# Queries turned on TensorE, key groups of nine tiles, exponentials summed on GpSimd, shared load buffers and a new searched order

## The chip, the cores and the metric

The kernel runs on one core of one Trainium2 chip. The metric is the device time of one execution in microseconds; the number quoted for a kernel is the median of its runs. The span that a profile covers is about 2 us shorter than the time of the same run, because the time includes what lies outside the first and last recorded instruction.

## The reference

Four batches of 12,544 rows of 128 numbers go through "agent attention" (49 agent rows stand between queries and keys), and the result through a feed-forward stage that takes the maximum of three linear layers of width 768.

```python
def _attn_ref(q, k, v, agents):           # q, k, v: (4, 12544, 128); agents: (4, 49, 128)
    ...                                    # sm(a, b): softmax over b of a @ b.T / sqrt(128)
    agent_v = sm(agents, k) @ v            # 49 x 128 per batch: needs ALL keys of the batch
    return sm(q, agents) @ agent_v

def _moe_ref(x, w1, w2, w3, w_out):        # x: (50176, 128), w1..w3: 128 x 768, w_out: 768 x 128
    h = np.maximum(np.maximum(x @ w1, x @ w2), x @ w3)
    return h @ w_out
```

The result of a query needs the finished `agent_v` of its batch. So keys of batch b+1 are worked on while queries of batch b are, and each batch change has to wait for a small calculation that ends the keys.

## The kernel before

A tile is 128 rows. Queries come in 49 groups of eight tiles, keys in groups of eight. For each batch a matrix `G` is made once from `agent_v` and the differences of the weights. After that a query group needs only: scores against 49 agents, one exponential (`e_q`), 12 products of `e_q` with `G` into three large PSUM buffers (`uv`), maxima of pairs of them (`a_sb` on ACT, `r` on DVE), the output products and a scale by the reciprocal sums.

The program is one list of small steps, each with a number that says when it is issued. One query group takes 6.0 of these numbers, whatever the time is. The table `KEY` holds the numbers inside a group; it was found by a search.

```python
    KEY = {"s": -0.90, "ex": -0.41, "u0": 0.94, ..., "rec": 3.76, ..., "sc1": 13.45}
    loads = ctx.enter_context(tc.tile_pool(name="loads", bufs=4))
    ...
    def uv_tile(dtype=FP32):     # three buffers of two banks: hidden products
        return psum.tile([P, 2, 512 ...], dtype, tag="uv", bufs=3, name="uv_ps")
    def small_tile(name, ...):   # two buffers of one bank: scores, sums, outputs
        return psum.tile([P, 512 ...], dtype, tag="om", bufs=2, name=name)
```

The parts of a key group that the change touches. The values and the sums of exponentials both come out of TensorE, the sums as a product with a matrix of ones:

```python
        def values():
            for j in reversed(range(n)):
                ...
                nc.tensor.matmul(t[:, c:c + A], d["vb"][:, j, :], e, ...)
                nc.tensor.matmul(t[:, c + A:c + 2 * A], ones, e, ...)
        def accumulate():        # DVE: values and sums, 98 columns
            nc.vector.tensor_tensor(out=Eacc[b], in0=d["s"][:, c:c + 2 * A], in1=Eacc[b], op=ALU.add)
        ...
            at(key - 22, load); at(key - 11, cast); at(key - 6.5, transposes)     # kT by DMA
```

At a batch change, normalisation, product and its two copies come together, just ahead of the new batch's first query:

```python
    def k_tail(b, key):
        def normalise(): ...     # DVE: reciprocal of the sums, avT = values * reciprocal
        at(key, normalise)
        at(key + 0.02, lambda: product(C31, WC, False))     # PE, copy by ACT
        at(key + 0.04, lambda: product(C21, C31, True))     # PE, copy by DVE
```

A query group's tiles are cast on GpSimd and turned (rows to columns) by DMA. Its sums share a small PSUM buffer, the "host", with a key group's scores:

```python
        def transposes():
            d["qT"] = work.tile([P, GT, P], BF16, tag="qT", bufs=3, name="qT")
            nc.sync.dma_start_transpose(out=d["qT"], in_=d["qb"].rearrange("p j c -> p (j c)"))
        ...
        at(key - 24, load); at(key - 13, cast); at(key - 9, transposes)
        at(key + KEY["s"], scores); at(key + KEY["ex"], exps); at(key + KEY["rec"], recips)
```

The softmax here doesn't subtract the row's maximum and nothing guards it: scores larger than these inputs give would overflow.

## Time and profile before

| | before |
|---|---|
| median of 3 runs, us | 517.82 (512.89 to 519.4) |
| profiled run, us; its span | 512.98; 511.0 |
| mean granted TensorE clock in it | 0.937 |
| 49 query exponentials, first and last start | 59.62 and 493.33 |

Engines are PE (TensorE), PEld (its weight loads), DVE (VectorE), ACT (ScalarE), POOL (GpSimd) and SP (SyncE, here the queue that issues the transfers). L214 is line 214 of the kernel's program. Two lines of the page of the kernel before show work that the change removes. The first is a group of instructions: count, busy us, mean ns of one, then the idle time of the engine ahead of them. The second is a kind of DMA issue: count, then median us from issue to landing.

```profile
L217 PE MATMUL m_ps<-e_k,ones 128*128 128x49 bf16 x392 | 30.0, 193 | 0.0
...
qT<-q_bf SPq DMA_TRANSPOSE x49, 6.9
```

A matmul's 193 ns is its whole passage; matmuls are pipelined, so they start far closer together than that (about 25 ns apart at 147.28 us of this trace).

### The profile page before, as it was taken

To read this page: it belongs to the slowest core of one execution; us is meant where nothing else is said; L and a number is where in the kernel's file an instruction comes from. 1 tells how busy PE (TensorE), PEld (TensorE's weight loads), DVE (VectorE), ACT (ScalarE), POOL (GpSimd) and SP (SyncE) were. 2 spreads that over 40 slices of the span, in tenths; PEclk is the share of its full clock that TensorE was granted. 3 is DMA by queue.
4 is the path that set the end of the run, shared out by engine and by line. 5 is a ranking of instruction groups with operands and counts; after the bars stand their busy time and mean duration, and the time that the engine had idled before them with its cause. 6 is when DMAs were issued, how large, how long until landed. Compare 5 with 4: busy or idle time off the path is not lost.

```text
span 511.0 us, 13285 instructions
## 1 busy us (share of the span) xinstructions
PE 450.0 (88%) x5426; PEld 277.5 (54%) x5426; DVE 391.5 (77%) x488; ACT 404.4 (79%) x463; POOL 141.3 (28%) x142
## 2 busy tenths in 40 slices
PE   2576499999999899999979899999998999999995
PEld 1464235556555565555545566555655555555554
DVE  2333168889888688888858579888888798998995
ACT  2554378898889689898859588989898898999993
POOL 2335534243342332432232433423211001110000
PEclk9985559999999899999979789999999999999998
DMA  8899999999999999999999999999984364663612
GB/s 324 304 411 402 307 287 280 289 296 252 302 308 283 256 293 292 299 252 279 260 254 294 296 253 338 272 266 269 235 228 139 104 206 139 173 160 110 124 58 110
DMA packets 121992, 127.78 MB, mean 250 GB/s; under 512 B 93959, under 2 KB 95947, under 8 KB 121931
## 3 DMA queue, kind: packets, MB, share of 16 engines
q1 hardware_dynamic: 120512, 125.26, 89.4%
q10 hardware_dynamic: 1419, 1.67, 0.9%
q8 instruction: 42, 0.69, 0.6%
q14 instruction: 19, 0.16, 0.1%
HBM read 78.74 MB, written 25.69 MB: 204 GB/s over the span
## 4 chain that ended last, share of the span: by engine, by line
DMA 47%; PE 22%; SPq 14%; POOL 8%; DVE 4%; issue 3%; ACT 1%; ACTq 0%; POOLq 0%; DVEq 0%
DMA v_st<-in_v_dram 25%; DMA k_st<-in_k_dram 16%; PE uv_ps L346 9%; PE o_ps L385 9%; SPq L188 7%; SPq L305 4%; POOL v_bf L179 4%; DVE r L371 3%; POOL k_bf L174 3%; DMA q_st<-in_q_dram 3%; SPq L167 3%; DMA wst<-in_moe_w_dram 2%; PE o_ps L376 2%; DMA kT<-k_bf 1%; PE m_ps L319 1%
## 5 line engine op out<-in xcount | busy, mean ns | idle before, releaser
L371 DVE TENSOR_TENSOR r<-uv_ps,a_sb 128x1024 bf16<-128x1024 f32 x245 | 295.2, 1222 | 54.6 <-PE uv_ps L346 46.5
L361 ACT ACTIVATE a_sb<-uv_ps 128x1024 bf16<-128x1024 f32 x245 | 244.8, 1024 | 32.0 <-PE uv_ps L346 28.3
L346 PE MATMUL uv_ps<-e_q,G 49*128 49x512 bf16 (+3 forms) x1248 | 198.0, 383 | 4.2 <-ACT G L276 1.4
L385 PE MATMUL o_ps<-wo_bf,r 128*128 128x128 bf16 x2352 | 192.8, 223 | 0.0
L385 PEld LDWEIGHTS <-r 128*128 128x128 bf16 x2352 | 143.8, 99 | 69.4 <-issue 66.7
L309 POOL CAST q_bf<-q_st 128x1024 bf16<-128x1024 f32 x49 | 51.0, 1042 | 242.0 <-DMA q_st<-in_q_dram 241.8
L346 PEld LDWEIGHTS <-G 49*128 49x128 bf16 x1248 | 56.2, 95 | 57.6 <-issue 26.7
L392 DVE TENSOR_TENSOR o_sb<-o_ps,recips 128x512 f32<-128x512 f32 x98 | 66.0, 674 | 14.4 <-PE o_ps L385 10.7
L174 POOL CAST k_bf<-k_st 128x1024 bf16<-128x1024 f32 (+2 forms) x50 | 51.2, 1025 | 53.5 <-DMA k_st<-in_k_dram 48.1
L358 ACT ACTIVATE uv_ps<-uv_ps 128x1024 f32<-128x1024 f32 x49 | 49.5, 1011 | 11.5 <-PE uv_ps L346 11.0
L369 ACT ACTIVATE r<-uv_ps 128x1024 bf16<-128x1024 f32 x49 | 50.2, 1024 | 8.3 <-PE uv_ps L346 3.8
L179 POOL CAST v_bf<-v_st 128x1024 bf16<-128x1024 f32 (+1 forms) x37 | 38.3, 1036 | 26.5 <-DMA v_st<-in_v_dram 16.5
L214 PE MATMUL m_ps<-e_k,v_bf 128*128 128x49 bf16 x392 | 30.0, 194 | 13.5 <-DVE recips L340 12.6
L376 PE MATMUL o_ps<-G,e_q 128*128 128x256 bf16 x196 | 38.8, 281 | 0.0
L217 PEld LDWEIGHTS <-ones 128*128 128x128 bf16 x392 | 25.7, 103 | 17.6 <-issue 17.6
L325 ACT ACTIVATE e_q<-m_ps 128x512 bf16<-128x512 f32 x49 | 29.0, 592 | 6.7 <-PE m_ps L319 6.7
L217 PE MATMUL m_ps<-e_k,ones 128*128 128x49 bf16 x392 | 30.0, 193 | 0.0
L177 ACT ACTIVATE v_bf<-v_st 128x1024 bf16<-128x1024 f32 (+1 forms) x13 | 13.1, 1007 | 19.9 <-DMA v_st<-in_v_dram 19.9
L204 ACT ACTIVATE e_k<-m_ps 128x392 bf16<-128x392 f32 (+2 forms) x50 | 24.3, 485 | 5.5 <-PE m_ps L199 5.5
L214 PEld LDWEIGHTS <-v_bf 128*128 128x128 bf16 x392 | 27.3, 103 | 0.5 <-issue 0.5
L319 PE MATMUL m_ps<-qT,agT 128*64 128x512 bf16 (+3 forms) x104 | 20.8, 407 | 6.0 <-DMA qT<-q_bf 6.0
L186 PE MATMUL uv_ps<-ident,k_bf 128*128 128x128 bf16 x98 | 12.0, 296 | 15.4 <-POOL k_bf L174 15.4
(46 smaller groups left out, 149.6 us busy)
## 6 DMA issues: line engine op xcount, KB each, us to landing
k_st<-in_k_dram SPq DMA_DIRECT2D x46, 512.0 KB, 5.5
v_st<-in_v_dram SPq DMA_DIRECT2D x46, 512.0 KB, 6.7
q_st<-in_q_dram SPq DMA_DIRECT2D x46, 512.0 KB, 4.0
out_dram<-o_sb SPq DMA_DIRECT2D x46, 512.0 KB, 6.1
wst<-in_moe_w_dram ACTq DMA_DIRECT2D x3, 384.0 KB, 7.9
qT<-q_bf SPq DMA_TRANSPOSE x49, 6.9
k_st<-in_k_dram SPq DMA_DIRECT2D x2, 384.0 KB, 6.6
v_st<-in_v_dram SPq DMA_DIRECT2D x2, 384.0 KB, 7.2
```

The costliest lines, as they stand in the source:

```text
L174: nc.gpsimd.tensor_copy(out=d["kb"][:, :n, :], in_=d["k"][:, :n, :])
L179: nc.gpsimd.tensor_copy(out=d["vb"][:, :n, :], in_=d["v"][:, :n, :])
L214: nc.tensor.matmul(t[:, c:c + A], d["vb"][:, j, :], e, start=(len(parts) > 1 and j == n - 1), stop=True, skip_group_check=True)
L217: nc.tensor.matmul(t[:, c + A:c + 2 * A], ones, e, start=False, stop=True, skip_group_check=True)
L309: nc.gpsimd.tensor_copy(out=d["qb"], in_=d["q"])
L346: nc.tensor.matmul(t[:, h, j0 * P:j1 * P], G[b][h * H:h * H + A, col + f * P:col + (f + 1) * P], d["e"][h * H:h * H + A, j0 * P:j1 * P], s ...
L358: nc.scalar.activation(u, u, AF.Relu)
L361: nc.scalar.activation(a_sb[f], u, AF.Relu)
L369: nc.scalar.activation(r, uv[f], AF.Relu)
L371: nc.vector.tensor_tensor(out=r, in0=uv[f], in1=a_sb[f], op=ALU.max)
L385: nc.tensor.matmul(t[:, c:c + C], r_sb[f][:, h, jj * P:(jj + 1) * P], wo_bf[:, f, :], start=False, stop=True, skip_group_check=True)
L392: nc.vector.tensor_tensor(out=d["out"][:, j:j + m, :], in0=d["o", o].rearrange("p (j c) -> p j c", c=C), in1=d["r"][:, j:j + m].unsqueeze( ...
```

## The change

It has five parts. Queries are turned by eight PE transposes and a DVE copy instead of a DMA transpose. Key groups have nine tiles, never cross a batch, and so number 11 a batch: in each batch of 12.25 query groups one beat carries no keys. Sums of exponentials are added up elementwise on GpSimd and reduced once a batch, so the matmuls against ones go; the normalisation then moves a beat ahead of the product. All loads share 14 buffers of one size. The numbers in `KEY`, and with them the leads of loads and casts, are new. Smaller moves come along: the weights are loaded by the sync queue, the early key scores sit in the large PSUM buffers, and the first key groups have other leads.

```diff
-    FI = NF - 1
-    NK = -(-NT // GT)
+    FI = 4
+    KT = 9
+    NK = -(-NT // KT)
     KEY = {
-        "s": -0.90, "ex": -0.41, "u0": 0.94, ... "rec": 3.76, ... "sc1": 13.45,
+        "qt": -2.57, "qe": -2.16, "s": -0.90, "ex": -0.20, ... "rec": 1.21, ... "ke": 2.10, ... "sc1": 15.54,
     }
-    loads = ctx.enter_context(tc.tile_pool(name="loads", bufs=4))
+    loads = ctx.enter_context(tc.tile_pool(name="loads", bufs=14))
     ...
         def values():
-            ...
-                nc.tensor.matmul(t[:, c + A:c + 2 * A], ones, e, start=False, stop=True, ...)
+            for j in range(n):
+                nc.tensor.matmul(d["s"][:, CV:CV + A], d["vb"][:, j, :], d["e"][:, j * A:(j + 1) * A], ...)
+        def add_exps():
+            if t0:
+                nc.gpsimd.tensor_tensor(out=Eacc[b][:, :n * A], in0=Eacc[b][:, :n * A],
+                                        in1=d["e"][:, :n * A], op=ALU.add)
     ...
-        at(key, normalise)
+        at(sum_key, reduce)
+        at(sum_key + 0.5, total)
+        at(sum_key + 1, normalise)          # sum_key lies in the query group before
     ...
-        def transposes():
-            nc.sync.dma_start_transpose(out=d["qT"], in_=d["qb"].rearrange("p j c -> p (j c)"))
+        def turn_q():
+            t = d["qT_ps"] = small_tile("m_ps", BF16)
+            for j in range(n):
+                nc.tensor.transpose(t[:, j * P:(j + 1) * P], d["qb"][:, j, :], ident)
+        def evacuate():
+            nc.vector.tensor_copy(out=d["qT"].rearrange("p j c -> p (j c)"), in_=d["qT_ps"])
     ...
-        at(key - 24, load)
-        at(key - 13, cast)
-        at(key - 9, transposes)
+        at(key + KEY["qt"] - 20, load)
+        at(key + KEY["qt"] - 7, cast)
+        at(key + KEY["qt"], turn_q)
+        at(key + KEY["qe"], evacuate)
```

## The prediction

> **What bounds the kernel now.** I read the page's busy strip first, then the chain of waits, then the exponentials of the query groups in order of time, because each of the 49 groups has exactly one of them and so they beat like a clock. The strip of the kernel before:
>
> ```profile
> PE   2576499999999899999979899999998999999995
> DVE  2333168889888688888858579888888798998995
> ACT  2554378898889689898859588989898898999993
> DMA  8899999999999999999999999999984364663612
> ...
> DMA 47%; PE 22%; SPq 14%; POOL 8%; DVE 4%; issue 3%; ACT 1%; ACTq 0%; POOLq 0%; DVEq 0%
> ```
>
> One character is 12.8 us. There are three stages. For about 60 us keys and values of batch 0 come in and the compute engines are a third busy. Then up to about 393 us 36 query groups run beside the key groups of batches 1 to 3, with the DMA full. Then 12 groups run with no keys and the DMA half empty. The chain says DMA 47%. That tempts one to call the middle stage DMA bound. The time order of the exponentials says otherwise (start us, us, engine line; middle stage with one batch change, then last stage):
>
> ```profile
> 158.12 0.59 ACT L325 ACTIVATE e_q<-m_ps 128x512 bf16<-128x512 f32 x1
> 166.84 0.59 ACT L325 ACTIVATE e_q<-m_ps 128x512 bf16<-128x512 f32 x1
> 171.49 1.02 ACT L276 ACTIVATE G<-uv_ps 128x1024 bf16<-128x1024 f32 x1 [2.90 <-PE uv_ps L269]
> 180.04 0.59 ACT L325 ACTIVATE e_q<-m_ps 128x512 bf16<-128x512 f32 x1
> ...
> 445.07 0.59 ACT L325 ACTIVATE e_q<-m_ps 128x512 bf16<-128x512 f32 x1
> 453.12 0.59 ACT L325 ACTIVATE e_q<-m_ps 128x512 bf16<-128x512 f32 x1
> 461.16 0.59 ACT L325 ACTIVATE e_q<-m_ps 128x512 bf16<-128x512 f32 x1
> ```
>
> The middle beats at 8.71 us and the last stage at 8.04 us, to a hundredth. Transfers do not keep such a beat; the order of instructions on PE, DVE and ACT does. The DMA is only just able to follow, and falls behind in places (around 250 to 300 us gaps of 11.2 and 11.7 us). So the span is: first exponential at 59.6 us, plus 48 intervals that make 433.7 us, plus 17.7 us from the last one to the end (493.3 to 511.0). At the two beats the 48 intervals would be 36 x 8.715 + 12 x 8.04 = 410.2; the other 23.5 us are the ramp (2.5), three batch changes (4.5, 6.4 and about 3) and DMA lateness. The load per beat, from the windows (us, then PE, PEld, DVE, ACT, POOL busy, clock, DMA share, GB/s):
>
> ```profile
> 120.00:160.00 40.00, 38.13 (x488) 23.58 (x488) 34.65 (x43) 35.75 (x42) 14.59 (x14) 1.00 1.08 300
> 440.00:480.00 40.00, 39.67 (x410) 22.26 (x409) 36.28 (x40) 36.96 (x41) 3.13 (x3) 1.00 0.56 139
> ```
>
> Scaled to one beat: middle ACT 35.75 x 8.715/40 = 7.79, DVE 7.55; last stage ACT 7.43, DVE 7.29. No engine is full: 0.6 to 0.9 us of each beat is the order's own waiting. PE's 95 to 99% is not its limit, since matmul ends are modelled; start to start in one beat (8 output matmuls in 0.46 us, 4 hidden ones in 0.54) I add up about 6.9 us without keys, 7.5 with.
>
> **What the Trainium skill says.** "TensorE: Matmul & The Clock Gate", Part 4, says a PE transpose ends in PSUM, needs a DVE copy after it, and takes about 275 ns in a kernel; the trace agrees (the early key transposes: 296 ns mean, but only 0.77 us of weight loads for eight, as they overlap). "VectorE: DVE Perf Modes", The TRN2 errata, gives 120 + FD/Accel cycles for PSUM to SBUF: (120 + 512)/0.96 = 658 ns for 1024 bf16; the trace has 691 for just this copy (kT from uv_ps). "GPSIMD Engine Reference", 3.1, puts a two-input add at about 2.6 cycles an element: for 441 columns an estimate of 0.96 us; no such instruction is in the trace. "DMA: Bandwidth & Descriptors", Latency and other measured facts, gives a DMA transpose 261 GB/s. The trace disagrees: at 400 to 440 us the DMA share is 0.58, 4.66 us a beat, of which the query load and store (1.05 MB at 385 GB/s, the rate of the first 40 us at full share) are 2.7; the other 1.9 us are the 256 KB transpose, some 135 GB/s. The measurement decides.
>
> **The change part by part.** The instruction order of the new kernel, which needs no run, confirms the counts.
> - Removed: 49 query DMA transposes, 1.9 us of DMA each. Middle beat now: 4 x 0.52 MB / 385 = 5.45, plus two transposes 3.7 = about 9.1 of 8.7 (share 1.08). After: (1.18 x 33/35 + 1.05) MB / 385 = 5.6, plus one transpose of nine tiles 1.8 to 2 = 7.5. The DMA gets out of the way, and the sync queue loses a 1.7 us issue per beat.
> - Added for it: 49 x 8 PE transposes, 0.46 us a beat, and 49 DVE copies of 0.69 us, 34 us in all. These hit every beat, the last stage too.
> - Removed: 392 matmuls against ones, about 25 ns each start to start, so 0.2 us a middle beat. PE's matmul count is thus the same, but 49 columns become 128. The DVE accumulate falls from 98 to 49 columns (0.26 to about 0.2).
> - Key groups of nine: 11 per batch, 33 beats with keys instead of 36, so 15 intervals without. GpSimd gets 44 adds of about 1 us; it is 28% busy and far from a bound.
> - New sums: middle DVE 7.55 + 0.69 - 0.06 = 8.18, ACT 7.79 + 0.04 = 7.83, PE 7.5 + 0.46 - 0.15 = 7.8. Without keys DVE 7.29 + 0.69 = 7.98, ACT 7.43. **DVE becomes the tightest engine**, and its sum is a floor.
> - The order: I walked one new beat by hand with trace durations (ACT 1.02, DVE max 1.15 to 1.21, PE pair to consumer 0.45). Each of the eleven uses of the three uv buffers waits for the consumer three uses back. DVE comes out nearly gapless and ACT waits about 0.5 us once: 8.3 us. Hand walks are kind, so I take 8.45 with keys and 8.2 without: 33 x 8.45 + 15 x 8.2 = 401.9.
> - Batch changes: normalisation now runs a beat ahead, so only the product and its two copies (1.03 ACT, 0.96 DVE) and a bubble remain: 3 us each, 9 in all, instead of about 14.
> - Start: before, the first query load lay behind 28 key and value loads and their waits for casts and landed at 62 us. Now 14 buffers let loads run ahead: weights 1.6 + batch 0 12.9 MB end at about 40 us, product matrix at about 48. But the first key transpose of batch 1 is issued behind three sets of q, k, v loads: 19.5 MB / 385 = 51 us, landing near 56, and PE meets its scores right after the first hidden matmul. I call the effective start 54 instead of 59.6.
> - End: same work, 17.7.
> Sum: 54 + 401.9 + 9 + 17.7 = 482.6 us of span. The profiled run before was timed 1.9 us over its span (512.98 against 511.0) and the median lies 4.9 over the fastest; I add 3.4 in all: **486 us**.
>
> **Rivals.**
> - DVE as new bound, worse than walked: a DVE at 8.2 of 8.45 has no room, and five tiles a beat instead of four now share two small PSUM buffers. At 8.8 with keys and 8.6 without (today's waiting of 0.6 on the new DVE sum): 33 x 0.35 + 15 x 0.4 = +17.6, about 503. For it: today's orders leave 0.6 to 0.9. Against: the order was searched again for just these operations.
> - The DMA was the true bound: then the middle beat falls towards what compute allows anyway and all lateness goes; near 474. For it: share 1.08 and 47% of the chain. Against: the constant 8.71.
> - The transposes were hidden and nothing is won but the start: beats stay 8.7 and 8.04, about 490; the added DVE copy speaks against 8.04 being kept.
> - PE clock falls when PE waits: early windows show 0.52 while PE starves. With PE over 90% busy after the start I expect 1.00.
>
> **Range and chances.** All but the slow walk lie between 474 and 490; the slow one reaches 503. Range 472 to 503. Two per cent of 517.8 is 507.5, above every rival, and even against the fast 512.9 the limit is 502.6. Faster 0.90, same 0.08, slower 0.02.
>
> **What would show it.** Beat of the query exponentials with keys near 8.45 and without near 8.2 (this must rise from 8.04); DVE busy at 95% or more in middle windows; DMA share there from 1.08 to below 0.95; copies qT from m_ps 49 x 0.69; GpSimd adds near 1 us; first a_sb activation at about 49 us with a gap soon after that ends on kT; intervals at batch changes near 11.5. Wrong if DVE waits remain as today, if two small buffers make PE wait on qT copies, if the adds on GpSimd delay the casts, or if the start stays at 60.

## The result, and the profile after

| | before | after |
|---|---|---|
| median of 4 runs, us | 518.61 (512.89 to 523.08) | 484.69 (484.52 to 485.66) |
| profiled span, us | 511.0 | 482.8 |
| mean granted TensorE clock | 0.937 | 0.971 |

The ratio of times is 0.938, 95% interval 0.931 to 0.946. A ratio here is the mean time of one kernel's fast runs over the mean of the other's fast runs of the same rounds, so it is not quite the ratio of the medians quoted. One run of the kernel before (523.08) lies 2% above its fastest, counts as slow and is not in the ratio. The kernel after is 6.2% faster and also steadier: its runs spread by 0.2%, the fast ones before by 1.3%. On other occasions the kernel before had medians of 512.68 and 514.65, so small differences between kernels are read below from beats inside the traces, not from its times.

The busy strip of the kernel after (40 equal slices, tenths) and its chain of waits:

```profile
PE   2464799999999999999998999999999999999996
DVE  2353579999999899999999899999999999999995
DMA  8999998897988899997988799994622424241213
...
PE 61%; DVE 15%; issue 9%; DMA 7%; ACT 6%; POOL 1%; SPq 0%; ACTq 0%; DVEq 0%; POOLq 0%
```

The dips in DVE's strip have gone, and the chain has turned from 47% DMA to 61% PE. A middle window of the kernel after (columns as in the prediction) and two groups that are new:

```profile
80.00:120.00 40.00, 39.30 (x515) 24.66 (x515) 37.90 (x50) 36.38 (x44) 20.11 (x20) 1.00 0.88 267
```

```profile
L328 DVE COPY qT<-m_ps 128x1024 bf16<-128x1024 bf16 x49 | 33.3, 681 | 3.5 <-PE m_ps L324 3.5
L209 POOL TENSOR_TENSOR Eacc<-Eacc,e_k 128x441 f32<-128x441 f32 x36 | 37.6, 1045 | 126.2 <-ACT e_k L193 126.2
```

DVE is 95% busy, the DMA share has fallen to 0.88, the copy takes 681 ns and an add on GpSimd 1,045 ns. The timeline of ACT in the kernel after around the first batch change:

```profile
146.20 0.60 ACT L340 ACTIVATE e_q<-m_ps 128x512 bf16<-128x512 f32 x1
...
155.49 0.60 ACT L340 ACTIVATE e_q<-m_ps 128x512 bf16<-128x512 f32 x1
...
158.74 1.02 ACT L273 ACTIVATE G<-uv_ps 128x1024 bf16<-128x1024 f32 x1 [0.71 <-PE uv_ps L266]
...
166.11 0.60 ACT L340 ACTIVATE e_q<-m_ps 128x512 bf16<-128x512 f32 x1
```

Before, ACT waited 2.90 us for the product and the interval was 13.20. Now it waits 0.71, and the two intervals around the change are 9.29 and 10.62.

**Where the 28.2 us went**, from the starts of the query exponentials in the two traces. The medians differ by 33.9 us: the profiled run before was one of its fastest, and what its longer runs spend more is not explained here. An ordinary beat with keys is 8.715 us before and 8.485 after; without keys 8.04 and 8.06.

| part of the span | before | after | difference |
|---|---|---|---|
| start to the fourth exponential | 88.2 | 78.4 | -9.8 |
| 45 ordinary beats (before 33 with keys and 12 without, after 30 and 15) | 384.1 | 375.5 | -8.6 |
| three batch changes, what their intervals have over the beats | 14.5 | 9.6 | -4.9 |
| late intervals (irregular, over the beat) | 6.5 | 0 | -6.5 |
| last exponential to the end | 17.7 | 19.4 | +1.7 |

Of the 8.6, 30 x 0.23 = 6.9 are the shorter beat, about 2.0 are three beats that lost their keys, and 0.2 goes the other way.

### The profile page after: what moved, and what is told of

Read it like the earlier page. It is cut to its first block, busy times and chain, and to the rows that moved or that the text cites. A ratio compares the mean times of both kernels' runs of the same rounds, so it can differ in the third digit from the quotient of the medians.

```text
span 482.8 us, 13241 instructions
## 1 busy us (share of the span) xinstructions
PE 435.4 (90%) x5434; PEld 275.3 (57%) x5434; DVE 415.9 (86%) x531; ACT 399.0 (83%) x455; POOL 177.0 (37%) x176
## 4 chain that ended last, share of the span: by engine, by line
PE 61%; DVE 15%; issue 9%; DMA 7%; ACT 6%; POOL 1%; SPq 0%; ACTq 0%; DVEq 0%; POOLq 0%
PE o_ps L399 24%; PE uv_ps L360 21%; DVE r L385 6%; DVE o_sb L406 5%; PE m_ps L324 5%; ACT e_k L193 4%; DMA st<-in_v_dram 4%; PE m_ps L334 3%; PE o_ps L390 3%; PE m_ps L197 3%; DMA st<-in_k_dram 2%; DMA kT<-k_bf 2%; DVE recips L354 1%; ACT a_sb L375 1%; ACT G L273 1%
## 5 line engine op out<-in xcount | busy, mean ns | idle before, releaser
L385 DVE TENSOR_TENSOR r<-uv_ps,a_sb 128x1024 bf16<-128x1024 f32 x245 | 296.7, 1217 | 19.3 <-PE uv_ps L360 15.8
L360 PE MATMUL uv_ps<-e_q,G 49*128 49x512 bf16 (+3 forms) x1248 | 182.3, 374 | 5.4 <-DVE r L385 2.6
L399 PE MATMUL o_ps<-wo_bf,r 128*128 128x128 bf16 x2352 | 179.4, 220 | 0.0
L209 POOL TENSOR_TENSOR Eacc<-Eacc,e_k 128x441 f32<-128x441 f32 (+1 forms) x40 | 41.3, 1034 | 143.4 <-ACT e_k L193 143.4
L319 POOL CAST q_bf<-st 128x1024 bf16<-128x1024 f32 x49 | 51.0, 1040 | 73.7 <-PE m_ps L324 73.7
L162 POOL CAST k_bf<-st 128x1152 bf16<-128x1152 f32 (+1 forms) x44 | 50.7, 1152 | 15.8 <-DMA st<-in_k_dram 15.0
L169 POOL CAST v_bf<-st 128x1152 bf16<-128x1152 f32 (+1 forms) x33 | 37.5, 1135 | 0.0
L328 DVE COPY qT<-m_ps 128x1024 bf16<-128x1024 bf16 x49 | 33.3, 681 | 3.5 <-PE m_ps L324 3.5
L324 PE MATMUL m_ps<-ident,q_bf 128*128 128x128 bf16 x392 | 31.2, 225 | 1.6 <-POOL q_bf L319 1.6
L324 PEld LDWEIGHTS <-q_bf 128*128 128x128 bf16 x392 | 24.8, 100 | 2.9 <-POOL q_bf L319 1.7
L197 PEld LDWEIGHTS <-v_bf 128*128 128x128 bf16 x392 | 16.6, 100 | 16.5 <-issue 13.0
L167 ACT ACTIVATE v_bf<-st 128x1152 bf16<-128x1152 f32 (+1 forms) x11 | 12.7, 1151 | 16.2 <-DMA st<-in_v_dram 16.2
```

Source lines behind the costliest of these rows:

```text
L162: nc.gpsimd.tensor_copy(out=d["kb"][:, :n, :], in_=d["k"][:, :n, :])
L209: nc.gpsimd.tensor_tensor(out=Eacc[b][:, :n * A], in0=Eacc[b][:, :n * A], in1=d["e"][:, :n * A], op=ALU.add)
L319: nc.gpsimd.tensor_copy(out=d["qb"], in_=d["q"])
L324: nc.tensor.transpose(t[:, j * P:(j + 1) * P], d["qb"][:, j, :], ident)
L360: nc.tensor.matmul(t[:, h, j0 * P:j1 * P], G[b][h * H:h * H + A, col + f * P:col + (f + 1) * P], d["e"][h * H:h * H + A, j0 * P:j1 * P], s ...
L385: nc.vector.tensor_tensor(out=r, in0=uv[f], in1=a_sb[f], op=ALU.max)
```

## The experiments

All ran on the same chip type with the kernel before beside them. The kernel after was not run again; a2 (484.99 us) and c2 (485.34), on the two chips used, lie within 0.2% of its 484.69, so differences of a few us from it can be read. Three groups: parts undone in the kernel after (names that begin with a, and d1), parts done alone in the kernel before (b), and attempts to go further (c). "Beat" is the ordinary interval between query exponentials with keys.

### a1: queries turned by DMA again

```diff
         def turn_q():
-            t = d["qT_ps"] = small_tile("m_ps", BF16)
-            ... eight transposes, and evacuate() ...
+            d["qT"] = work.tile([P, GT, P], BF16, tag="qT", bufs=3, name="qT")
+            nc.sync.dma_start_transpose(out=d["qT"], in_=d["qb"].rearrange("p j c -> p (j c)"))
...
+        at(key - 24, load); at(key - 13, cast); at(key - 9, turn_q)      # leads as before
```

> The changed kernel with one part undone: queries turned by DMA again, no transposes on PE and no copy on DVE. Theory (DMA relief is what the turn on PE buys): in beats with keys the DMA must do about 9.4 us (5.6 of copies, 1.9 for the query transpose, 1.9 for the key transpose) while the order wants about 8.4, so the beats go to 8.8 to 9.3 and become uneven, DMA share over 1.0; beats without keys fall below 8.06; total 495 to 505 us. Rival (the DMA never bound; the turn is only a cost and the new order is the gain): beats with keys fall to 8.0 to 8.2, total about 470 us.

Measured: 488.61 us (488.09 to 489.32), span 487.3, ratio to before 0.953. Neither expectation held. The beat is 8.465, practically that of the kernel after, though the window of the same stage shows DVE relieved and the DMA over full again:

```profile
80.00:120.00 40.00, 38.49 (x466) 22.17 (x464) 34.82 (x44) 36.57 (x43) 20.52 (x20) 1.00 1.04 294
```

So in the beats of a1 the DMA bounds nothing at a share of 1.04 (1.10 in 200 to 240 us), and in those of the kernel after the DVE bounds nothing by being 95% busy. The beats without keys hardly move either: 8.04, against 8.06. Where the 0.45 us of transposes went shows in the chain of one beat of a1, where PE waits for an `a_sb` of ACT:

```profile
210.33 0.34 PE uv_ps L355 x2
210.68 0.02 issue
210.70 1.03 ACT a_sb L370
211.73 0.04 issue
211.77 0.39 PE uv_ps L355 x2
```

These five pieces take 1.83 us. In the kernel after the same stretch holds four hidden matmuls, four output ones, eight transposes and four hidden ones, 1.86 us. The transposes fill a wait of PE that would be there anyway. a1 loses 4.5 us of span against the kernel after: 5.3 at the start, less what the beats give. There PE stands still for a query transpose:

```profile
53.57 0.64 PE L329 MATMUL m_ps<-qT,agT 128*64 128x512 bf16 x2 [10.57 <-DMA qT<-q_bf]
```

The fourth exponential comes at 83.7 us instead of 78.4.

### a2: three pools of four load buffers instead of 14 shared

```diff
-        return loads.tile([P, KT, C], FP32, tag="st", name="st")
+        return loads.tile([P, KT, C], FP32, tag=f"{kind}_st", bufs=4, name=f"{kind}_st")
```

> The changed kernel with its 14 shared load buffers replaced by three pools of four, as before the change. Theory: only the start suffers, since four pairs of key and value tiles are in flight instead of seven; beats stay 8.49 and 8.06; total 486 to 491 us. Rival (the deep buffers carry the middle stage over late transfers): beats with keys become uneven and the total goes over 495. Second rival (the buffers do nothing): 484 to 485.5 us.

Measured: 484.99 us (484.43 to 485.74), span 483.3. The beats and the start are those of the kernel after to 0.5 us. The deep shared buffers buy nothing.

### a3 and a4: the DVE copy twice, the transposes twice

```diff
+            for _ in range(2):
                 nc.vector.tensor_copy(out=d["qT"].rearrange("p j c -> p (j c)"), in_=d["qT_ps"])
```

> The changed kernel with the copy of the turned queries done twice on DVE (the same result). Theory (DVE is the tightest engine, 8.0 to 8.2 us of work in a beat of 8.49): each of 49 beats grows by nearly the 0.6 us of a copy, total 508 to 516 us. Rival (PE is the tightest, as its 61% of the chain suggests; DVE has room): less than 10 us more, under 495 us.

```diff
-            for j in range(n):
+            for j in list(range(n)) * 2:
                 nc.tensor.transpose(t[:, j * P:(j + 1) * P], d["qb"][:, j, :], ident)
```

> The changed kernel with the eight query transposes done twice on PE (the same result): 0.46 us more on PE in each beat. Theory (DVE bound): the transposes lie where PE has some slack, total grows by 3 to 10 us, 488 to 495. Rival (PE bound): 49 x 0.46 = 22 us more, about 507 us.

Measured: a3 510.21 us, span 508.3, beat 9.01 (+0.52). a4 504.97 us, span 504.5, beat 8.93 (+0.44). By its total a3 looks like a kernel that DVE bounds, and a4 like one that PE bounds. A second copy costs three quarters of its 0.68 us in each beat, a second set of transposes all of its 0.44. Yet the first of both, together, cost 0.02 (a1). The chain of a beat in the kernel after explains a4:

```profile
107.45 0.55 ACT e_k L193
108.00 0.04 issue
108.04 0.39 PE m_ps L197 x9
...
109.97 0.45 PE m_ps L324 x8
...
113.04 0.79 PE o_ps L399 x12
113.83 0.03 issue
113.87 0.59 DVE o_sb L406
114.46 0.04 issue
114.50 0.06 DVE r L385
114.56 1.08 issue
115.64 0.21 DVE recips L354
...
115.94 0.55 ACT e_k L193
```

From `e_k` to `e_k` it is 8.49 us, the beat. The key exponential (0.55) releases the value matmuls. PE then runs without a gap for 5.79 us, the transposes (L324) in it. DVE scales an output and takes a maximum (the "issue" of 1.08 is the rest of that maximum). Then comes the small reciprocal of the query sums, `recips`, and only after that may the next `e_k` start. The beat is a **circle of waits through three engines**: 0.59 ACT, 5.79 PE, 1.98 DVE and 0.13 of handovers. No engine has to be full for it. In a4 the chain has `m_ps L324 x16` with 0.89 us in place of 0.45.

The copy is not in this chain. In a3 the chain of a beat has changed and runs through both copies:

```profile
206.26 0.69 DVE o_sb L407
206.95 0.61 DVE qT L329
207.56 0.02 issue
207.58 0.03 DVE qT L329
207.62 0.57 issue
208.19 1.22 DVE r L386
```

The 0.57 of "issue" is the rest of the second copy. So the first copy fits into time in which DVE waits, the second no longer does, and another circle, 9.01 us long, takes over.

Why does `e_k` wait for `recips` at all? They work on different columns, but both read one PSUM bank, that of the host; that is the likely reason. The Trainium skill, "PSUM — Partial Sum Buffer", PSUM bank collisions raise a hardware error, says that two engines must not access one bank in the same quadrant at once, whichever columns they touch, and that a program has to order them. The trace agrees that the order exists: ACT's `e_k` starts 0.10 us after the end of DVE's `recips`. No run here tried what happens without it.

### a5: no adds on GpSimd after a batch's first (wrong result)

```diff
-            if t0:
-                nc.gpsimd.tensor_tensor(out=Eacc[b][:, :n * A], ..., op=ALU.add)
-            else:
+            if not t0:
```

> The changed kernel without the adds of exponentials on GpSimd after the first of each batch (the result is wrong on purpose: the sums are too small). Theory (GpSimd is off the path, 37% busy): beats unchanged, only the start loses about 1 us of adds ahead of the first product; 483 to 485 us. Rival (the adds hold up the casts): beats fall below 8.4, under 480 us.

Measured: 483.62 us (482.92 to 484.15), span 481.1, beat 8.42; relative error 9.9, as it must be. The adds cost 0.06 us a beat and 1 to 2 us in all. GpSimd is off the path nearly everywhere. One warning: the record of the clock shows 1.00 in this trace from the start, while eight transposes at 57.03 us took 1.04 us, as they do at a recorded 0.50 in the kernel after. In the kernel before eight at 14.65 us took 1.03 at a recorded 1.00. So the mean clocks quoted here are somewhat too high.

### d1: the normalisation back in the beat of the product

```diff
-        at(sum_key + 0.5, total)
-        at(sum_key + 1, normalise)
+        at(sum_key + 0.002, total)          # batch 0 stays as it was
+        at(sum_key + 0.004, normalise)
...
-        hosting.add(s - 1)
-        k_tail(b, 6.0 * (s - 1) + KEY["ho"] + 0.001, 6.0 * s + KEY["u0"] - 0.15, s - 1)
+        hosting.add(s)
+        k_tail(b, 6.0 * s + KEY["ho"] + 0.001, 6.0 * s + KEY["u0"] - 0.15, s)
```

> The changed kernel with the reduce, total and normalise of a finished batch moved from a beat ahead to just ahead of the product at the batch change, as the kernel before has it; nothing else. Theory (most of what groups of nine and GpSimd sums buy is that the normalisation runs a beat early): each of three batch changes grows from 3.3 us over the beats to 6 to 7.5, total 493 to 497 us. Rival (the batch change costs what the product and its copies cost, wherever the normalisation stands): under 488 us.

Measured: 490.09 us (487.58 to 491.93), profiled span 485.8, the lowest of its four runs. It is 3.0 us longer by span and 5.4 by the medians. The three changes in the profiled run went from 3.3, 3.3 and 3.0 us over the beats to 5.0, 4.1 and 3.9. Right in direction, smaller than expected.

### b2: 14 shared load buffers in the kernel before

```diff
-                t = loads.tile([P, GT, C], FP32, tag=f"{name}_st", bufs=4, name=f"{name}_st")
+                t = loads.tile([P, GT, C], FP32, tag="st", bufs=14, name="st")       # q_st likewise
```

> The kernel before with 14 shared load buffers alone. Theory (buffers do nothing for the beats; a little for the start): 507 to 515 us, beats 8.71 and 8.04. Rival (loads that come late cause the uneven intervals of the kernel before between 250 and 310 us and its spread between runs): those go, total 500 to 506 and spread under 2 us.

Measured: 515.42 us (512.81 to 517.8), ratio 1.005 (0.998 to 1.013). Nothing, as in a2.

### b3: the new order alone; b4: the new order and queries turned on TensorE

b3 puts the new `KEY` and `FI = 4` (with the weight differences that go with it) into the kernel before; the transfers and casts keep their old distance to their users. b4 adds `turn_q` and `evacuate` as in the change.

```diff
-    FI = NF - 1
+    FI = 4
-    KEY = { ... old ... }
+    KEY = { ... new ... }
-            at(key - 22, load)
-            at(key - 11, cast)
-            at(key - 6.5, transposes)
+            at(key + KEY["ks"] - 24, load)
+            at(key + KEY["ks"] - 13, cast)
+            at(key + KEY["ks"] - 8.6, transposes)
```

> The kernel before with one part of the change alone: the new searched order (and relu feature 4 in place of 5, which the order asks for). Queries still turned by DMA, groups of eight with sums by ones matmuls, own load pools. Theory after the first four runs (the beat is a cycle of waits in the order, not the DMA): beats with keys 8.5, without 8.04, batch changes 3 us instead of 4.5 to 6.4, start still near 60; total 491 to 497 us. Rival (the DMA bounds the middle of the kernel before): beats stay at 8.7 or become uneven, total over 505 us.

> The kernel before with the new order and the queries turned on TensorE, but groups of eight with ones matmuls and own load pools as before. Theory: beats as in b3_new_order within 0.1 us (16 value and ones matmuls instead of 9 lengthen the cycle a little), the start about 5 us earlier as the first query no longer waits for a DMA transpose behind queued loads; 486 to 491 us. Rival (groups of nine and sums on GpSimd carry much of the gain): over 495 us.

Measured: b3 509.38 us (508.31 to 510.83), span 506.5; b4 503.77 us (503.36 to 504.48), span 501.8. Both are slower than expected, and b4 as slow as its rival said (over 495), though the beats did what was hoped: 8.53 in b3 and 8.55 in b4, and all but one of b3's late intervals are gone while the queries are still turned by DMA. What gave the gain back are the batch changes, with intervals of 14.7 to 16.2 us in b3 and 14.1 to 15.5 in b4. The timelines of DVE and PE in b4 at the first change show why:

```profile
162.24 2.36 DVE L375 TENSOR_TENSOR r<-uv_ps,a_sb 128x1024 bf16<-128x1024 f32 x2
164.52 0.45 DVE L253 RECIPROCAL k_recip<-Eacc 128x49 f32<-128x49 f32 x1
164.93 0.09 DVE L255 MEMSET avT<- 128x32 uint32 x1
165.04 0.21 DVE L256 TENSOR_TENSOR avT<-Eacc,k_recip 128x49 bf16<-128x49 f32 x1
```

```profile
165.31 1.61 PE L268 MATMUL uv_ps<-wall,avT 128*64 128x512 bf16 x10 [2.96 <-DVE avT L256]
```

The normalisation sits on DVE behind two maxima of the old batch's last hidden tiles, and PE stands for 2.96 us. In the kernel after the same reciprocal was done at 150.44 us, eight microseconds ahead of the product. So the new order needs the normalisation a beat ahead; by itself it is worth little (ratio 0.995, 0.988 to 1.001).

By span, the steps before, b3, b4, after are 511.0, 506.5, 501.8, 482.8. The last step, 19.0 us, splits into changes 19.3 to 9.6 (-9.7), start 83.1 to 78.4 (-4.7), 30 beats of 8.555 to 8.485 (-2.1), three beats without keys (-1.5) and late intervals (-1.0). The buffers are not in it (a2, b2); of the 9.7, d1 gives back 3 to 5. The rest of the 9.7 I put down to groups that do not cross a batch: with 11 of nine, a batch's last values are ready more than a beat before the change, while groups of eight run up to it. That part is argued, not shown by a run. For the 4.7 at the start the trace of b4 offers a reason, which no run tests either. Groups of eight leave six tiles of batch 1 ahead of the first query, turned by DMA, and PE stands for them:

```profile
53.76 0.43 PE L198 MATMUL m_ps<-agT,kT 128*128 128x49 bf16 x6 [4.53 <-DMA kT<-k_bf]
```

Only after them come the first query's transposes, at 55.24 us. The kernel after has no such group; its first query is turned at 44.01 us, while the last keys of batch 0 are still worked on.

### c1: the reciprocals after the key exponential

If the circle of waits is right, moving `recips` behind `e_k` opens it.

```diff
-        "sum": 0.95, "rec": 1.21,
+        "sum": 0.95, "rec": 2.60,
```

> The changed kernel with one number of the order changed: the reciprocal of the query sums at 2.60 instead of 1.21, behind the fifth max of a beat. In the chain of waits of a beat with keys the key exponential on ACT waits for this reciprocal on DVE. Theory (the beat is this cycle: value matmuls, a run of PE, scale, max, reciprocal, exponential): beats with keys fall by 0.1 to 0.2 to 8.3 or 8.4, beats without keys stay 8.06; total 478 to 482 us. Rival (DVE or PE work sets the beat): 8.48 stays, 484 to 485 us.

Measured: 479.94 us (479.0 to 480.77), six runs, span 478.2, ratio to before 0.933 (0.930 to 0.936). The beat falls to 8.29. First ACT, then the chain of one beat of c1:

```profile
209.85 0.56 ACT L193 ACTIVATE e_k<-m_ps 128x441 bf16<-128x441 f32 x1
```

```profile
209.69 0.90 PE uv_ps L360 x6
210.59 0.34 PE m_ps L197 x9
210.92 0.67 PE o_ps L399 x12
```

`e_k` follows the activation before it at once, without a wait, and the value matmuls (L197) run with no gap after the hidden ones. In this window of 20 us the chain has nothing but PE. With the circle open, PE's own sequence is the bound, and it is 8.29 us long. b4 agrees: its chain is PE alone too, with 0.56 us of value and ones matmuls for the 0.34 here, and its beat is 8.555. One number in a table beats both kernels.

The page of the kernel before had shown this wait already. In its line of the value matmuls, 12.6 us of PE's idle time end with the same reciprocal (in 33 waits, 0.38 us each):

```profile
L214 PE MATMUL m_ps<-e_k,v_bf 128*128 128x49 bf16 x392 | 30.0, 194 | 13.5 <-DVE recips L340 12.6
```

No run moves `recips` in the kernel before.

### c2 and c3: later loads and a warm clock at the start

At the start of the kernel after, PE waits for the key transpose that the prediction named. The first two lines are its chain, the last two windows of PE (busy us, clock, DMA share, GB/s):

```profile
45.07 8.75 DMA kT<-k_bf
53.81 0.05 issue
```

```profile
56.00:58.00 2.00, 2.00 (x14) 0.50 1.93 333
...
68.00:70.00 2.00, 2.00 (x18) 0.71 1.01 406
```

The granted clock is 0.50 from 42 to 68 us, although PE is recorded as busy nearly throughout from 54. Eight transposes at 56.89 us take 1.04 us, at 118.30 us 0.61. c2 issues the prefetching loads later, so that the key transpose comes earlier in the queue, and fills PE's idle time with products of the identity that nobody reads. c3 is c1 and c2 together.

```diff
-            at(key + KEY["ks"] - 22, load)
+            at(key + KEY["ks"] - 17, load)
-        at(key + KEY["qt"] - 20, load)
+        at(key + KEY["qt"] - 14, load)
+    def warm(t, n):
+        for _ in range(n):
+            nc.tensor.matmul(t[:, :P], ident, ident, start=True, stop=True, skip_group_check=True)
     # 18 to 28 of these (or transposes) ahead of the late transposes, total, product, first hidden
```

> The changed kernel with two changes at the start: loads are issued later, so that the first key transpose by DMA stands behind two sets of loads instead of three, and idle PE before the first group is filled with dummy matmuls of the identity. Theory (the start waits for the first key transpose, landing at 53.8 us, and then PE runs its first two beats at half clock, eight transposes in 1.04 us): transpose lands near 49.5 us, the clock stays full, third exponential at 74 to 76 us instead of 78.4; beats unchanged; total 480 to 482.5 us. Rival one (dummies do not hold the clock): 482.5 to 484. Rival two (later loads make beats uneven): over 485 us.

> Both edits of c1_recips_late and c2_start. They touch different stages, so their gains should add: 474.5 to 479.5 us, below both kernels. Rival (either fails): 480 to 485 us.

Measured: c2 485.34 us (484.46 to 486.35), c3 479.59 (479.14 to 480.74): no gain in either, the 5.75 us between them is c1's again, now within one set of rounds. The wait for the key transpose is gone (scores right after the first hidden pair, at 55.36 us) and the clock held at 1.00 until 62 us. But the idle products held up the last key groups (last early `e_k` 44.94 instead of 42.16 us, `G` copied at 53.71 instead of 51.40), and the clock then fell all the same, between 62 and 64 us, after waits of PE of at most 0.6 us each from 52 us on, and stayed low where PE has no idle time. Two windows of PE in c2:

```profile
56.00:58.00 2.00, 1.20 (x17) 1.00 0.99 214
...
66.00:68.00 2.00, 2.00 (x15) 0.50 1.02 407
```

The fourth exponential came at 79.1 us, against 78.4. What the clock follows at the start stays open.

## Why the prediction was right, and where it was right by luck

The time was predicted as 486 (472 to 503) and measured as 484.69; the sum of spans as 482.6, measured 482.8. By its own terms:

| term | predicted | measured |
|---|---|---|
| effective start (fourth exponential less three beats) | 54 | 78.39 - 3 x 8.485 = 52.9 |
| beats with keys | 33 x 8.45 | 8.485 (33 x 0.035 = +1.2) |
| beats without | 15 x 8.2 | 8.06 (15 x -0.14 = -2.1) |
| batch changes | 9 | 9.6 |
| end | 17.7 | 19.4 |
| time over span | 3.4 | 1.9 |

No term is off by more than 2.1 us and they cancel. The reasons are less good than the terms: that 8.45 came so near to 8.485 is luck, since it was walked along DVE and the beat is set by other waits.

- **"DVE becomes the tightest engine, and its sum is a floor"** failed. The sum was near (8.18 predicted; 37.9 x 8.485 / 40 = 8.04 measured), but with the copy taken off DVE (a1) the beat stayed. The bound was a circle of waits. Below it lies PE, whose sequence takes 8.29 us in c1 and 8.55 with the matmuls against ones in b4, where the chain of a beat is PE alone too. My sum for PE was 7.8: the mis-sized term is the time of PE's sequence, which I added up from starts seen in one beat. Already its 7.5 for the kernel before was low, if the new order changes PE's own time little: b4's 8.555 less 0.45 for the transposes makes 8.1.
- **"Transfers do not keep such a beat"** was right, and a1 proves it better than I had argued: the DMA transposes come back, the share goes to 1.04 to 1.10, the beat does not move.
- **"The DMA gets out of the way"** was right as a share (predicted below 0.95; measured 0.88, 0.92 and 0.94 in three windows, but 1.01 in 280 to 320 us) and wrong as a gain in the beats. Turning on TensorE pays almost only at the start: 4.5 us of span in a1 undone, 4.7 from b3 to b4 done, 4.2 of these before the fourth exponential. Lateness mostly went with the order alone (b3).
- **"Now 14 buffers let loads run ahead"** failed: a2 and b2 show nothing. The reading under it was wrong too: the first query load of the kernel before landed by 47.0 us, where its cast starts, and 62 us is the fourth one's. The first exponential, at 59.62, waited for the query's DMA transpose, issued at 49.94. The start came earlier for other reasons, among them the query that no longer needs this transpose behind the loads.
- **The key transpose landing near 56 us and PE meeting its scores after the first hidden matmul** was right: it landed at 53.8. The first `a_sb`, however, came at 53.13 and not at 49.
- **The beat without keys must rise from 8.04** was nearly wrong: 8.06. The DVE copy hid in waits: a1, without it, has 8.04. In its chain DVE does a scale and a maximum (1.83 us) where before it did one maximum.
- **Batch changes at 3 us by the normalisation a beat ahead**: right in size (3.2 on average). d1 confirms the mechanism for 3 to 5 of the 9.7 us that the changes save against b4. The step left out that the new order makes the change worse unless that is done.
- **"End: same work, 17.7"** failed by 1.7 us: it comes with the order (19.8 in b3, 19.4 in b4). `KEY` has a group's last scale at 15.54 instead of 13.45; that nothing follows at the end to hide this delay is my reading, not shown by a run.
- **GpSimd far from a bound**: right, 0.06 us a beat (a5).

Of the rivals, "the transposes were hidden and nothing is won but the start" was the nearest to the truth for that part of the change; it missed the new order's beats.

## What to carry to other kernels

An engine that is 95% busy, or a DMA share over 1.0, need not be the bound: follow the chain through one beat and back to the instruction it began with, and if it passes through several engines, look for a step that is in the circle only by its place in the order. Doubling a step tells what one more would cost; only removing it tells what the first one costs, and here that was 0.44 and 0.52 us a beat against 0.02. A searched order suits the program that it was searched for: put into the old program alone it gained 0.5%, which is not clear of noise, because what it gave in each beat it took at the batch changes.

## What the Trainium skill lacked or had wrong

- "TensorE: Matmul & The Clock Gate", Part 1, What's actually happening: it says the clock is released after about 3.4 us of sustained activity. In the kernel after, the granted clock stayed at 0.50 from 54 to 68 us with PE recorded as busy for about 13.6 of these 14 us, mostly with matmuls on 49 rows (about 2 us are transposes); in c2 a clock at 1.00 fell between 62 and 64 us, with PE 1.67 of 2.00 us busy, and stayed at 0.50 to 70 us with PE 2.00 of 2.00 busy. PE busy in the trace is modelled and may not be the activity that the clock follows; I found no page that says what share of the rows counts.
- "DMA: Bandwidth & Descriptors", Latency and other measured facts: 261 GB/s for a DMA transpose; the estimate from the DMA shares of the kernel before is 135 GB/s.
- "GPSIMD Engine Reference", 3.1: its 2.6 cycles an element give an estimate of 0.96 us for a two-input add of 441 columns, 8% low; 1,045 ns measured. The section names a cost of dispatching each instruction but gives no figure for it on GpSimd.
- No page that I read describes a beat set by a circle of waits between engines; here it was 8.485 us, with PE's own sequence 8.29 (c1).
